# First products issued a slot early, piece sums on VectorE, interleaved weight conversion

## The chip, the core and the metric

The kernel runs on one core of a Trainium2 chip. The metric is device time in microseconds (us) of the whole kernel: 945.47 us, the median of three runs (941.27, 945.47, 945.98).

## What is computed

Three layers, one after the other, in float32 on the outside:

```python
attn_out = _attn_ref(q, k, v)                    # 4 x 8 heads, 576 x 64, masked softmax
x = attn_out.transpose(0, 2, 1, 3).reshape(2304, 512)
h = x @ w_in;  x = (h * cos(h)) @ w_out          # 512 -> 2048 -> 512
g = x @ w_gate                                   # 512 -> 1536
val = x @ w_val
out = (g / (1 + exp(-g)) * val) @ w_out2         # 1536 -> 512
```

## The kernel before

**Number format.** Each float32 matrix is scaled and split into two float16 parts, and a product takes three float16 matmuls in a row (`mm3`, lines 532 to 534, or line 680). "hi" is the rounded part, written by ScalarE (`hi_part` L245, `piece_hi` L654), "lo" is the rest, written by VectorE (`lo_part` L248, `piece_lo` L657).

**Stages.** The 2304 tokens are cut into five blocks, three of 512 and two of 384 columns (`BLOCKS`). After attention, the first dense layer runs as 5 x 16 steps: `up1` multiplies by a slice of `w_in`, ScalarE and VectorE form h cos(h) in four steps that alternate between them (L565 ScalarE, L568 VectorE, L572 ScalarE, L575 VectorE), L579 and L580 (POOL) split the result, and some steps later `down1` multiplies it by `w_out` into four accumulators `acc0` to `acc3`. A product of `up1` stays in a PSUM bank (the pool `bank` has four) until L575 of that step has read it.

**The second layer** uses a scheme with seven products in place of eight for 2 x 2 blocks, in both directions. It runs as 30 **slots** (5 blocks x 6). A slot makes seven products of four `mm3` each (`multiply(k, ...)`) with slice j of the gate and value weights, in the order 0, 1, 5, 4, 6, 2, 3. Some add to a bank that already holds an earlier product; before that, ScalarE copies the earlier state out (`snap`, L1170), and VectorE adds copies and banks up (`join`, L1174). `px`, `py` and `pz` are the three banks of a slot. From the joined gate and value halves come, for each of two row halves, a tanh (L643, ScalarE) and two VectorE steps (`silu`, L649 and L650). The first half is done inside its slot, the second half in the next slot. Then POOL forms four sums of quarters (`piece_sums`, L665), and hi and lo parts of the seven pieces are written (`first_set`: one piece; `second_set`: two; `third_set`: the four sums).

From slot 6 on, products of the block before with `w_out2` (`lower`, L680, seven a slot) fill TensorE between the products of a slot. They accumulate in `acc0` to `acc3` in turn (`k % KC`); `quarter_out` (L697, L703) empties them. In slots 0 to 5 there are none, except that slot 0 still has four `down1`. After slot 29 a **tail** of 42 `lower` for the last block remains.

**Work beside it.** Conversion of weights is kept in a list `fill`. Each item has a cost by hand, and `pump(share)` takes items until a budget is used up; in the first layer the budget is `SHARE` (0.95) of a step's slack in blocks 0 and 1 and `SHARE2` (0.77) from block `SB` = 2 on. The gate and value weights come first (POOL sums L902), then `w_out2`: twelve raw tiles of two 32-bit words a number, in six rounds j of two tiles. A round is `conv` (L224 ScalarE, L231 and L235 VectorE, for both tiles, then four sums on POOL, L323), `tops` (three hi parts in a row, ScalarE), `ends` (three lo parts, then `third`: a scaled copy of 1792 columns, L342, and the store to DRAM). All ScalarE items have cost 0, so that `pump` emits them in one go with the next item that has a cost.

A second list, `urgent`, holds for each block the scaling and splitting of the activations; `pump_urgent` takes one item. For the second layer these are eight **fold** items a block: items 0, 1, 5 and 6 contain a VectorE subtraction (L602), items 0 to 6 a hi part on ScalarE, items 1 to 7 a lo part on VectorE. The hi parts of items 5 and 6 read the difference of the same item. They are taken in slots 2 to 4 (three, three, two), and in the same place of the blocks that follow.

**What sets the order.** Every engine runs its own instructions in the order of emission; nothing is reordered by a scheduler. DMAs are issued on the SP queue in order of emission too. `load_w2` fetches slices of `w_out2` (576 KB) into the buffers in `w2_free`, `load_w7` a slot's gate and value weights (1792 KB) into one of three buffers.

## Time and profile before

| | |
|---|---|
| median of the three runs | 945.47 us |
| profiled execution, its own time | 940.64 us |
| span of its instructions | 938.9 us |
| TensorE busy | 870.9 us (93%) |
| VectorE busy | 669.8 us (71%) |
| ScalarE busy | 522.9 us (56%) |
| POOL busy | 301.3 us (32%) |

The span runs from the first to the last instruction of the profiled execution; its time is 1.7 us longer. Stretches below are given in us from the start of the span: the `w_out2` conversion lies in about 400 to 505, slots 0 to 5 in 518 to 603.7, slots 6 to 29 in 603.7 to 909, and the tail after that. A value in square brackets behind an instruction is the time for which its engine stood idle ahead of it and the instruction whose end released it.

### The profile page before, as it was taken

How to read it: one execution, taken by the hardware profiler on the slowest of the kernel's cores; microseconds unless marked ns; L12 is line 12 of the kernel's file. 1: busy time of each engine (PE TensorE's matmuls, PEld its weight loads, DVE VectorE, ACT ScalarE, POOL GpSimd, SP SyncE). 2: the span in 40 equal slices, each digit the busy share in tenths (PEclk: the TensorE clock that was granted, in tenths of full speed). 3: DMA queues.
4: the chain of work that ended last, by engine and by line, in shares of the span. 5: the costliest groups of instructions: out<-in, count | busy, mean ns of one | idle time of the engine just before them, and what ended most of it. 6: DMA issues, size and time to landing. Idle time of an engine off the chain costs nothing. (4 is left out here: it accounts for less than half of the span.)

```text
span 938.9 us, 18454 instructions
## 1 busy us (share of the span) xinstructions
PE 870.9 (93%) x7228; PEld 612.3 (65%) x7228; DVE 669.8 (71%) x1223; ACT 522.9 (56%) x1040; POOL 301.3 (32%) x367
## 2 busy tenths in 40 slices
PE   7999999989999799998789977899999999999997
PEld 4767644434444344554445666688888889999997
DVE  4898898976679979947686376657865775765662
ACT  4889888644365676546766455444434444444440
POOL 3344133112156656235452122212222122222220
PEclk7899999999999899999999997999999999999999
DMA  9998822475555746723545344457677768788866
GB/s 311 351 294 248 277 91 90 160 245 194 187 191 180 237 159 195 234 85 104 187 158 184 146 167 193 157 180 253 233 241 258 239 223 277 288 284 306 301 179 260
DMA packets 53511, 200.60 MB, mean 214 GB/s; under 512 B 5456, under 2 KB 16208, under 8 KB 49584
## 3 DMA queue, kind: packets, MB, share of 16 engines
q1 hardware_dynamic: 53424, 199.42, 62.3%
q8 instruction: 57, 0.93, 0.4%
q14 instruction: 30, 0.25, 0.1%
HBM read 175.41 MB, written 23.99 MB: 212 GB/s over the span
## 5 line engine op out<-in xcount | busy, mean ns | idle before, releaser
L532 PE MATMUL bank<-xs,wi 128*128 128x256 f16 (+3 forms) x860 | 258.3, 300 | 48.3 <-DVE tb L575 20.2
L533 PE MATMUL bank<-xs,wi 128*128 128x256 f16 (+3 forms) x860 | 258.0, 300 | 0.0
L534 PE MATMUL bank<-xs,wi 128*128 128x256 f16 (+3 forms) x860 | 257.8, 300 | 0.0
L580 POOL TENSOR_TENSOR arena<-tb,arena 128x512 f16<-128x512 f32 (+1 forms) x80 | 91.0, 1139 | 228.4 <-ACT arena L579 213.4
L533 PEld LDWEIGHTS <-wi 128*128 128x128 f16 x880 | 87.2, 99 | 91.1 <-issue 59.1
L665 POOL TENSOR_TENSOR wi<-tb 128x256 f32<-128x256 f32 (+1 forms) x60 | 40.6, 676 | 295.6 <-DVE tb L650 295.6
L533 PE MATMUL acc<-arena 128*128 128x512 f16 (+1 forms) x320 | 114.5, 358 | 0.4 <-POOL arena L580 0.4
L532 PE MATMUL acc<-arena 128*128 128x512 f16 (+1 forms) x320 | 114.5, 358 | 0.0
L534 PE MATMUL acc<-arena 128*128 128x512 f16 (+1 forms) x320 | 114.5, 358 | 0.0
L532 PEld LDWEIGHTS <-wi 128*128 128x128 f16 x880 | 87.3, 99 | 38.4 <-issue 3.8
L534 PEld LDWEIGHTS <-wi 128*128 128x128 f16 x880 | 87.4, 99 | 37.3 <-issue 3.0
L680 PEld LDWEIGHTS <-arena 128*128 128x128 f16 x1116 | 103.6, 98 | 8.6 <-DMA arena<-w 0.4
L1174 DVE TENSOR_TENSOR arena<-bank,cv 128x512 f32<-128x512 f32 (+1 forms) x90 | 57.0, 634 | 64.2 <-PE bank L534 56.7
L643 ACT ACTIVATE tb<-arena,c 128x512 f32<-128x512 f32 (+1 forms) x60 | 40.7, 679 | 95.8 <-DVE arena L1174 94.7
L565 ACT ACTIVATE tb<-bank,quarter,c 128x512 int32<-128x512 f32 (+1 forms) x75 | 54.4, 725 | 58.4 <-PE bank L534 42.3
L680 PE MATMUL acc<-arena 128*128 128x256 f16 (+1 forms) x750 | 86.3, 264 | 0.2 <-DMA arena<-w 0.2
L533 PEld LDWEIGHTS <-arena 128*128 128x128 f16 x600 | 59.0, 98 | 37.4 <-issue 4.5
L534 PEld LDWEIGHTS <-arena 128*128 128x128 f16 x600 | 59.0, 98 | 33.6 <-issue 0.6
L532 PEld LDWEIGHTS <-arena 128*128 128x128 f16 x600 | 59.0, 98 | 32.8
L532 PE MATMUL bank<-xs,arena 128*128 128x256 f16 (+1 forms) x280 | 74.1, 265 | 4.1 <-ACT cv L1170 4.1
L533 PE MATMUL bank<-xs,arena 128*128 128x256 f16 (+1 forms) x280 | 74.1, 265 | 0.0
L534 PE MATMUL bank<-xs,arena 128*128 128x256 f16 (+1 forms) x280 | 74.1, 265 | 0.0
(141 smaller groups left out, 1630.8 us busy)
## 6 DMA issues: line engine op xcount, KB each, us to landing
wi<-w SPq DMA_DIRECT2D x20, 1792.0 KB
arena<-w SPq DMA_DIRECT2D x62, 576.0 KB, 4.9
raw<-w_out SPq DMA_DIRECT2D x56, 512.0 KB, 4.3
arena<-w SPq DMA_DIRECT2D x10, 1792.0 KB
raw<-w_gate SPq DMA_DIRECT2D x24, 512.0 KB, 4.3
raw<-w_val SPq DMA_DIRECT2D x24, 512.0 KB, 5.0
w<-arena SPq DMA_DIRECT2D x42, 256.0 KB, 2.1
raw<-w_in SPq DMA_DIRECT2D x16, 512.0 KB
```

Source lines behind the costliest of these rows:

```text
L532: nc.tensor.matmul(out=o, lhsT=w[:, 0, c], rhs=x[0], start=first, stop=False, **kw)
L533: nc.tensor.matmul(out=o, lhsT=w[:, 0, c], rhs=x[1], start=False, stop=False, **kw)
L534: nc.tensor.matmul(out=o, lhsT=w[:, 1, c], rhs=x[0], start=False, stop=last, **kw)
L565: nc.scalar.activation(out=c["w"].bitcast(I32), in_=c["ph"], func=AF.Identity, scale=turn[c["blk"]], bias=quarter)
L580: nc.gpsimd.tensor_tensor(out=g[:, 1, 0:n], in0=w, in1=g[:, 0, 0:n], op=ALU.subtract)
L643: nc.scalar.activation(out=t, in_=c["C"][m][:, 0, 0:n], func=AF.Tanh, scale=half[c["blk"]])
L665: nc.gpsimd.tensor_tensor(out=to, in0=x, in1=y, op=ALU.subtract)
L680: nc.tensor.matmul(out=o[:, c], lhsT=w[:, 256 * i + 128 * c:256 * i + 128 * c + 128], rhs=unit(u)[:, x:x + h], start=j == c == i == 0, sto ...
L1174: nc.vector.tensor_tensor(out=c["C"][m][:, :, h * right:h * right + h], in0=p, in1=t, op=ALU.add)
```

## The change

Five edits.

1. **A slot's first product is issued a slot ahead.** `open_slot(s + 1)` takes a bank and issues product 0 of the next slot between products 6 and 3 of this one. The order inside a slot is now 1, 4, 5, 2, 6, (0 of the next slot), 3. `py` moves from the pool `bank` to `acc3`; `lower` therefore uses only `acc0` to `acc2` (`k % 3`), except for the first four products of the last block.
2. **Sums of pieces.** Three of the four sums of `piece_sums` move from POOL to VectorE. The first (`piece_first`) stays on POOL, a slot earlier, as soon as its inputs exist.
3. **The `w_out2` conversion** is cut into single steps and emitted with round j, j - 1 and j + 1 interleaved. Its four sums a round move from POOL to VectorE, with a cost of 0.45 each, and `third` is cut into 3 and 4 of 7 parts.
4. `SHARE2` rises from 0.77 to 0.85.
5. `load_w2` gets two freed weight buffers in slots 28 and 29 in place of after slot 29. The calls `pump(2.0)` and `pump(3.5)` in the slots are dropped; the list is empty there in both versions.

```diff
-SHARE, SHARE2, SB = 0.95, 0.77, 2
+SHARE, SHARE2, SB = 0.95, 0.85, 2
...
-                nc.gpsimd.tensor_tensor(out=sums[:, k], in0=x, in1=y, op=op)
+                nc.vector.tensor_tensor(out=sums[:, k], in0=x, in1=y, op=op)
...
+            def third(a, z):
+                nc.scalar.activation(out=stage[:, a:z, 512:768], in_=stage[:, a:z, 0:256], func=AF.Copy, scale=2.0 ** -11)
...
+                emit += now["fix"][0] + old["hi"][0:1] + now["fix"][1] + old["hi"][1:2] + now["sums"][0:2] + old["hi"][2:3]
+                emit += old["lo"][0:1] + now["sums"][2:4] + old["third"][0:1] + old["lo"][1:2] + new["conv"][0] + old["lo"][2:3]
+                emit += new["conv"][1] + old["third"][1:2] + old["store"]
...
-            for to, x, y in ((t1, b12, b11), (t3, b22, b12), (t2, b22, t1), (t4, b21, t2)):
-                nc.gpsimd.tensor_tensor(out=to, in0=x, in1=y, op=ALU.subtract)
+            for to, x, y in ((t2, b22, t1), (t3, b22, b12), (t4, b21, t2)):
+                nc.vector.tensor_tensor(out=to, in0=x, in1=y, op=ALU.subtract)
+
+        def piece_first(c):
+            h = c["n"] // 2
+            nc.gpsimd.tensor_tensor(out=t_sums[:, 0, 0:h], in0=c["t"][0][:, h:2 * h], in1=c["t"][0][:, 0:h], op=ALU.subtract)
...
-                acc_t[2, blk, k] = pacc.tile([128, 512], F32, name=f"acc{k % KC}")
+                acc_t[2, blk, k] = pacc.tile([128, 512], F32, name=f"acc{k if blk == NBLK - 1 and k < KC else k % 3}")
...
+        def open_slot(s):
+            blk, j = slots[s]
+            if j == 0:
+                need_urgent(("ys", blk))
+                up2_scales(blk)
+            h = BLOCKS[blk][1] // 2
+            p = halves(bank(), h)
+            multiply(0, w7_slots[s % W7S], ys[blk], p, h, True)
+            return p
...
+            if s + W7S > len(slots):
+                w2_free.extend(thirds((early_w[:, 0:14], early_w[:, 14:28], part(2 * HOMES, 14))[(s - 1) % W7S], 3))
+            if s == 4 or s + W7S > len(slots):
                 load_w2()
...
             a = snap(px)
+            while queue:
+                down_next()
+            py = halves(pacc.tile([128, 512], F32, name=f"acc{KC - 1}"), h)
             multiply(1, w, x, py, h, True)
             join(0, 0, py, a)
             if last:
+                piece_sums(last)
                 his, los = second_set(last)
                 run(his)
-            while queue:
-                down_next()
-            multiply(5, w, x, px, h, False)
-            a = snap(px)
+            pz = halves(bank(), h)
+            multiply(4, w, x, pz, h, True)
+            b = snap(pz)
             if last:
                 run(los)
             pump_urgent()
-            pz = halves(bank(), h)
-            multiply(4, w, x, pz, h, True)
-            b = snap(pz)
+            multiply(5, w, x, px, h, False)
+            a = snap(px)
...
-            multiply(6, w, x, px, h, False)
-            join(1, 1, px, b)
+            multiply(2, w, x, pz, h, False)
+            join(0, 1, pz, a)
             if last:
                 run(los)
             downs(2)
             pump_urgent()
-            pump(2.0)
-            multiply(2, w, x, pz, h, False)
-            join(0, 1, pz, a)
             t = gate_tanh(c, 0)
+            multiply(6, w, x, px, h, False)
+            join(1, 1, px, b)
             silu(c, 0, t)
             his, los = first_set(c)
             run(his)
+            piece_first(c)
             run(los)
+            old = px
+            if s + 1 < len(slots):
+                px = open_slot(s + 1)
             downs(3)
             pump_urgent()
-            pump(3.5)
-            multiply(3, w, x, px, h, False)
-            nc.scalar.activation(out=c["C"][1][:, :, 0:h], in_=px, func=AF.Copy)
+            multiply(3, w, x, old, h, False)
+            nc.scalar.activation(out=c["C"][1][:, :, 0:h], in_=old, func=AF.Copy)
```

**ScalarE in the conversion.** This is what stands between two steps of the first layer at a change of round before the change (L342 is `third`, L245 a hi part, L224 the first step of a tile, L565 the first step on a bank of `up1`):

```order
L342 ACTIVATE arena<-arena 128x7x256
L245 ACTIVATE arena<-raw,s_4741 128x256
L245 ACTIVATE arena<-raw,s_4741 128x2x256
L245 ACTIVATE arena<-arena,s_4741 128x4x256
L224 ACTIVATE raw<-raw 128x512
L565 ACTIVATE tb<-bank,quarter,c_4263 128x384
```

And this is what stands around one round's third and hi parts now (L336 is a part of `third`, L574, L588 and L581 are the steps that were L565, L579 and L572):

```order
L336 ACTIVATE arena<-arena 128x4x256
L245 ACTIVATE arena<-raw,s_4593 128x256
L574 ACTIVATE tb<-bank,quarter,c_4291 128x384
L588 ACTIVATE arena<-tb 128x384
L245 ACTIVATE xs<-xy_70,s_4719 128x384
L581 ACTIVATE tb<-tb,right 128x384
L245 ACTIVATE arena<-raw,s_4593 128x2x256
L574 ACTIVATE tb<-bank,quarter,c_4291 128x384
```

The block of `third`, three hi parts and the next tile's step, which stood ahead of L565 in a row, is spread over several steps of the first layer.

**TensorE between two slots.** The end of product 3 of slot 2 and the start of slot 3 before the change (weights from `arena` belong to slot 2, from `wi` to slot 3):

```order
L534 LDWEIGHTS arena_2101
L534 MATMUL bank_5931<-xs_5223,arena_2101 128x256
L532 LDWEIGHTS wi_71
L532 MATMUL bank_6055<-xs_5223,wi_71 128x256
L533 LDWEIGHTS wi_71
L533 MATMUL bank_6055<-xs_5223,wi_71 128x256
```

The same place now, one product earlier:

```order
L542 LDWEIGHTS wi_71
L542 MATMUL bank_6046<-xs_5235,wi_71 128x256
L543 LDWEIGHTS wi_71
L543 MATMUL bank_6046<-xs_5235,wi_71 128x256
L541 LDWEIGHTS arena_2101
L541 MATMUL bank_5924<-xs_5235,arena_2101 128x256
L542 LDWEIGHTS arena_2101
L542 MATMUL bank_5924<-xs_5235,arena_2101 128x256
```

Product 0 of slot 3 (bank_6046) is followed by product 3 of slot 2 (bank_5924), where it came after it.

**VectorE in a slot.** From the second half's silu to the last join of slot 1 before the change (L649 and L650 silu, L1174 join, L657 lo parts):

```order
L649 SCALAR_TENSOR_TENSOR tb<-tb,arena 128x512
L650 SCALAR_TENSOR_TENSOR tb<-tb,arena 128x512
L1174 TENSOR_TENSOR arena<-bank,cv 128x2x256
L657 SCALAR_TENSOR_TENSOR arena<-arena,tb 128x2x256
L1174 TENSOR_TENSOR arena<-bank,cv 128x2x256
L657 SCALAR_TENSOR_TENSOR arena<-arena,wi 128x4x256
L1174 TENSOR_TENSOR arena<-bank,cv 128x2x256
```

The same place now (L658 and L659 silu, L1190 join, L674 sums of pieces, L666 lo parts):

```order
L658 SCALAR_TENSOR_TENSOR tb<-tb,arena 128x512
L659 SCALAR_TENSOR_TENSOR tb<-tb,arena 128x512
L1190 TENSOR_TENSOR arena<-acc_5841,cv 128x2x256
L674 TENSOR_TENSOR wi<-tb,wi 128x256
L674 TENSOR_TENSOR wi<-tb 128x256
L674 TENSOR_TENSOR wi<-tb,wi 128x256
L666 SCALAR_TENSOR_TENSOR arena<-arena,tb 128x2x256
L1190 TENSOR_TENSOR arena<-bank,cv 128x2x256
```

Three sums stand between the first join and the lo parts, and the first join reads an accumulator in place of a bank.

**SP at the end.** Stores of the fourth block's output (L700) and loads of `w_out2` (L1102) around the last slots before the change:

```order
L700 DMA out<-xy_69 128x2x192
L1102 DMA arena<-w_0_2104 128x2304
L1102 DMA arena<-w_1_2105 128x2304
L700 DMA out<-xy_69 128x2x192
L1102 DMA arena<-w_0_2104 128x2304
L1102 DMA arena<-w_1_2105 128x2304
L700 DMA out<-xy_69 128x2x192
L1102 DMA wi<-w_0_2104 128x2304
```

And now (L713 and L1107):

```order
L1010 DMA arena<-w_5_2111 128x7168
L1107 DMA arena<-w_1_2105 128x2304
L1107 DMA arena<-w_0_2104 128x2304
L1107 DMA wi<-w_1_2105 128x2304
L1107 DMA wi<-w_0_2104 128x2304
L1107 DMA wi<-w_1_2105 128x2304
L1107 DMA arena<-w_0_2104 128x2304
L713 DMA out<-xy_69 128x2x192
```

The loads into `wi`, which came behind the last store of the fourth block, stand ahead of its second.

## Rows read from the trace of the kernel before

**Rows 1.** Windows: stretch, its us, busy us of PE, PEld, DVE, ACT, POOL; PEclk, DMA, GB/s
```profile
261.00:363.00 102.00, 95.48 (x433) 42.51 (x431) 89.72 (x139) 67.17 (x112) 59.46 (x58) 0.97 0.57 193
400.00:505.00 105.00, 88.67 (x510) 51.13 (x509) 70.19 (x125) 68.60 (x112) 47.30 (x46) 0.95 0.36 129
518.00:603.70 85.70, 70.77 (x568) 57.86 (x566) 51.38 (x80) 38.60 (x62) 20.16 (x24) 0.92 0.41 154
603.70:909.00 305.30, 296.43 (x3011) 275.05 (x3009) 202.19 (x334) 137.65 (x242) 75.41 (x96) 1.00 0.73 251
909.00:939.00 30.00, 23.26 (x258) 22.39 (x255) 8.74 (x15) 3.30 (x6) 2.52 (x4) 0.94 0.70 255
```

**Rows 2.** Waits of TensorE in 400 to 505: us in total, times, longest
```profile
PE bank L532 <- DVE tb L575: 14.2, 8, 3.8
```

**Rows 3.** Timeline: POOL's first of four sums, then ScalarE, TensorE
```profile
419.31 0.85 POOL L323 TENSOR_TENSOR arena<-raw 128x256 f32<-128x256 f32 x1 [1.78 <-DVE raw L235]
...
422.50 1.15 ACT L245 ACTIVATE arena<-arena,s 128x1024 f16<-128x1024 f32 x1 [2.48 <-POOL arena L323]
...
427.54 0.48 PE L532 MATMUL bank<-xs,wi 128*128 128x384 f16 x1 [3.83 <-DVE tb L575]
```

**Rows 4.** Timeline of ScalarE and VectorE at another change of round
```profile
449.37 1.69 ACT L342 ACTIVATE arena<-arena 128x1792 f16<-128x1792 f16 x1
...
453.74 0.43 DVE L231 TENSOR_SCALAR raw<-raw 128x512 int32<-128x512 int32 x1 [5.14 <-ACT raw L224]
```

**Rows 5.** Windows, of line 323 (POOL's sums) alone
```profile
400.00:505.00 105.00, 25.84 (x24) 0.95 0.36 129
```

**Rows 6.** Waits of TensorE in 518 to 604, then in 604 to 909
```profile
PE bank L532 <- ACT cv L1170: 14.8, 5, 4.4
...
PE bank L532 <- ACT cv L1170: 8.9, 8, 1.8
```

**Rows 7.** Timeline from slot 4 to slot 5, VectorE, ScalarE and TensorE
```profile
587.20 1.22 DVE L657 SCALAR_TENSOR_TENSOR arena<-arena,wi 128x1024 f16<-128x1024 f16 x1
...
588.99 0.68 DVE L1174 TENSOR_TENSOR arena<-bank,cv 128x512 f32<-128x512 f32 x1
589.71 0.72 ACT L643 ACTIVATE tb<-arena,c 128x512 f32<-128x512 f32 x1 [2.96 <-DVE arena L1174]
590.46 0.69 DVE L649 SCALAR_TENSOR_TENSOR tb<-tb,arena 128x512 f32<-128x512 f32 x1 [0.79 <-ACT tb L643]
...
591.91 0.42 ACT L654 ACTIVATE arena<-tb 128x256 f16<-128x256 f32 x1 [1.48 <-DVE tb L650]
...
593.48 0.58 ACT L1170 ACTIVATE cv<-bank 128x512 f32<-128x512 f32 x1
594.10 0.37 PE L532 MATMUL bank<-xs,arena 128*128 128x256 f16 x1 [2.38 <-ACT cv L1170]
```

**Rows 8.** Timeline of slot 4's folds: VectorE alone, then beside POOL
```profile
577.87 0.68 DVE L602 TENSOR_TENSOR wi<-xy 128x512 f32<-128x512 f32 x1
...
582.76 2.34 POOL L665 TENSOR_TENSOR wi<-tb,wi 128x256 f32<-128x256 f32 x2
583.30 1.22 DVE L602 TENSOR_TENSOR wi<-xy,wi 128x512 f32<-128x512 f32 x1
```

**Rows 9.** Windows of slots 1 to 5, of slot 2, of slot 3
```profile
535.30:602.40 67.10, 52.26 (x423) 43.71 (x421) 45.41 (x65) 33.03 (x54) 17.74 (x20) 0.90 0.46 173
546.90:558.00 11.10, 9.35 (x86) 8.22 (x85) 8.09 (x12) 6.86 (x11) 3.68 (x4) 1.00 0.48 167
558.00:574.00 16.00, 12.05 (x87) 9.50 (x85) 10.61 (x16) 7.43 (x12) 3.68 (x4) 0.79 0.31 116
```

**Rows 10.** Timeline: VectorE empties an accumulator of the first layer, slot 0
```profile
528.51 0.62 DVE L546 TENSOR_SCALAR xy<-acc,c 128x384 f32<-128x384 f32 x1 [0.36 <-PE acc L534]
```

**Rows 11.** Timeline of the tail: SP issues loads, TensorE waits
```profile
911.37 4.29 SPq L1102 DMA_DIRECT2D wi<-w  x6
...
917.44 0.67 PE L680 MATMUL acc<-arena,wi 128*128 128x192 f16 x6 [2.62 <-DMA wi<-w]
```

More of the change, by code (lines that the diff above doesn't have):

```diff
@@ L303, in direct_later, with seven_steps @@
             rests.append((0.7, lambda: lo_part(tiles[j][:, 1], box["c"], scale_w[mat][0], tiles[j][:, 0]), (mat, j)))
[L305 to L323 removed]
+        def seven_steps(j, stage, sums):
+            boxes, conv = [], []
+            for q in range(2):
+                box, steps = conv_steps("out2", 2 * j + q, None, False, lambda: None)
+                boxes.append(box)
+                conv.append(steps)
             def sources():
@@ L343, in third, with store @@
+            def store():
                 nc.sync.dma_start(out=w2_d[j // 3][:, :, j % 3].rearrange("q p n -> p q n"), in_=stage)
-            def tops():
-                for k in range(3):
-                    later(0, lambda k=k: hi(k))
-            def ends():
-                for k, cost in ((2, 1.25), (1, 0.7), (0, 0.45)):
-                    later(cost, lambda k=k: lo(k))
-                later(0, third, ("out2", j))
-            return conv, tops, ends
+            return dict(conv=[c[0:1] for c in conv], fix=[c[1:] for c in conv],
+                        sums=[(0.45, lambda k=k: combine(k)) for k in range(4)],
+                        hi=[(0, lambda k=k: hi(k)) for k in range(3)],
+                        lo=[(cost, lambda k=k: lo(k)) for k, cost in enumerate((0.45, 0.7, 1.25))],
+                        third=[(0, lambda: third(0, 3)), (0, lambda: third(3, 7))], store=[(0, store, ("out2", j))])
@@ new lines, in seven_later @@
+        def seven_later():
+            all_steps = [seven_steps(j, *stages[j % 2]) for j in range(NPR)]
+            none = dict(conv=[[], []], fix=[[], []], sums=[()] * 4, hi=[()] * 3, lo=[()] * 3, third=[()] * 2, store=[()])
+            emit = []
+            for a in all_steps[0]["conv"]:
+                emit += a
+            for j in range(NPR + 1):
+                now = all_steps[j] if j < NPR else none
+                old = all_steps[j - 1] if j else none
+                new = all_steps[j + 1] if j + 1 < NPR else none
+                emit += now["fix"][0] + old["hi"][0:1] + now["fix"][1] + old["hi"][1:2] + now["sums"][0:2] + old["hi"][2:3]
+                emit += old["lo"][0:1] + now["sums"][2:4] + old["third"][0:1] + old["lo"][1:2] + new["conv"][0] + old["lo"][2:3]
+                emit += new["conv"][1] + old["third"][1:2] + old["store"]
+            for step in emit:
+                if step:
+                    later(*step)
@@ L944, in open_weights @@
                 scale_later("out2", TW_LAST)
-                ends = None
-                for j in range(NPR):
-                    conv, tops_, next_ends = seven_later(j, *stages[j % 2])
-                    conv()
-                    if ends:
-                        ends()
-                    tops_()
-                    ends = next_ends
-                ends()
+                seven_later()
         opened, most = [], [HOMES]
@@ L1147, in build @@
             h = n // 2
-            if j == 0:
-                need_urgent(("ys", blk))
-                up2_scales(blk)
             if s == 1:
@@ L1228, in build @@
         blk = NBLK - 1
-        for i in range(len(slots) - W7S, len(slots) - 1):
-            w2_free.extend(thirds((early_w[:, 0:14], early_w[:, 14:28], part(2 * HOMES, 14))[i % W7S], 3))
         c_last[blk] = prod(c_o[blk], scale_w["out2"][1])
```

32 lines of the change are left out of this document (8 added, 24 removed).

## The prediction

> **What bounds the kernel now.** I read the busy time by stretch first, then who TensorE waited for in each, then the timeline in front of the longest waits. TensorE is the bound: it is busy 93% of the span, and from 604 to 909 it works 296.4 of 305.3 us [rows 1]. So the change can only win TensorE's idle time and what the low clock level costs. That sits in four places, all read from [rows 1, 2, 6, 11]. In the conversion (400 to 505) TensorE idles 105 - 88.7 = 16.3 us, 14.2 of them for VectorE's L575, which frees the bank, and a mean granted clock of 0.95 costs about 0.05 x 105 = 5.2 us more. In slots 0 to 5 it waits 14.8 us for ScalarE's copy L1170, and 0.08 x 85.7 = 6.9 us go to the clock. In slots 6 to 29 it waits 8.9 us for the same copy. In the tail it waits 2.6 us for a load, and 0.06 x 30 = 1.8 us go to the clock. Together 55 us; the question is how much of each place comes back.
>
> **The conversion (edits 2 and 3).** Two things hold up the bank. Four sums run on POOL one after the other, from 419.31 on; the hi part of the sums waits for them 2.48 us on ScalarE, and the four-step chain on the banks is queued behind it, so TensorE starts 3.83 us late [rows 3]. At another round ScalarE does `third` (1.69), three hi parts and the next tile's step in a row, and VectorE sits idle for 5.14 us [rows 4]. Both go: the order shows the ScalarE burst spread over several steps, and the sums come a round ahead of their use. What is new: 24 sums on VectorE. No row has one of 256 columns there; the nearest has 512 columns and takes 0.68 us [rows 8], so each costs between 0 and 0.68, and I take 0.40, near half: 24 x 0.40 = 9.6 us. VectorE is busy 70.2 us in a stretch that would shrink to some 91 us: (70.2 + 9.6) / 91 = 88%; ScalarE 68.6 / 91 = 75%. Neither is the bound by itself, but both are full enough for some waits to stay. The common scales and the two-chain cross waits stay as well. I keep 4 of the 14.2 us and a quarter of the clock's 5.2: **gain 10.2 + 3.9 = 14 us**, bounds 4 (VectorE full) and 18 (all but the scales).
>
> **SHARE2 (edit 4)** moves work, it adds none. In block 2 VectorE is already busy 89.7 of 102 us and TensorE loses 6.5 [rows 1]. About a tenth more conversion a step fills VectorE further there and empties block 3. I take **0**, bounds -5 (about the loss that is there doubled) and +4.
>
> **Slots 0 to 5 (edits 1 and 2).** The wait is a chain, readable from slot 4 to slot 5 [rows 7]: after product 2, join (588.99, 0.68), tanh (0.72), silu (twice 0.69), hi part (0.42), copy of product 3, tanh of the second half (0.72 again), copy of `px` (593.48, 0.58), and only then product 5. From 588.99 to 594.06 that is 5.1 us. Beside it TensorE has products 3, 0 and 1, and a product takes 9.35 / 7 = 1.3 us [rows 9], so 3.9 us: TensorE waits. After the change five products stand between 2 and the next 5 (6, 0 of the next slot, 3, 1, 4), 6.6 us. The chain gets longer too, because the lo part of the third set (1.22 for 1024 columns) and the join after product 6 (0.68) stand ahead of silu on VectorE: I work it out to some 6.1 us after product 2. It fits, barely. One new wait appears: the copy of `pz` is queued on ScalarE behind the second set's hi parts, which wait for silu, so product 2 starts about 0.4 us late. A slot without folds thus takes 7 x 1.31 + 0.4 = 9.6 us.
>
> Slots with folds are worse. VectorE has to do the three sums (1.2 us) and, in slots 2 to 4, up to three fold items of 0.7 to 1.4 us, and the join that product 3 waits for is queued behind one of them: about 1.4 us of wait in slot 2, 0.9 in slot 3. In slot 4 the hi part of fold item 6 needs its own VectorE subtraction and stands on ScalarE ahead of the copy that frees `px` for product 6. There I count four waits, of 1.7, 0.8, 1.7 and 0.8 us. That makes slots of 11.0, 11.2 and 14.1 us, and 9.6 and 10.1 us for slots 1 and 5: 56 us against 67.1 now [rows 9], a gain of 11. Slot 0 gives 0.6 back: product 1 goes to `acc3` and must wait until VectorE has emptied it (0.62 us after the last `down1`) [rows 10]. I leave 1.5 us for one stretch of the low clock. **Gain 9 us**, bounds 2 and 15. The sums cost VectorE 1.2 us a slot, but POOL's sums stretch its work now: L602 takes 0.68 us alone and 1.22 beside L665 [rows 8], so most of that comes back in slots with folds.
>
> **Slots 6 to 29.** Seven `lower` a slot, 0.67 us each by the tail's row [rows 11], add 4.7 us of cover; about five of them lie over the chain, so it has 6.6 + 3.3 = 9.9 us of TensorE work beside it, and the fold slots still fit. Of 8.9 us I keep 3.9: **gain 5**, bounds 1 and 7. Three accumulators in place of four cost nothing within a block, since two whole products lie between two uses of one.
>
> **The tail (edit 5).** Six loads are issued at 911.37, and TensorE waits for one until 917.44 [rows 11]. SP's order has them two slots earlier, over 10 us. The wait of 2.6 us and most of the low clock after it go. Against that, `acc0` now holds both the fourth block's last product and the first one of the tail, and the `quarter_out` between them comes behind silu: about 0.7 us. **Gain 3.5**, bounds 2 and 4.5. Piece loads of SP queued behind these early ones have a slot's time of slack.
>
> **The sum:** 14 + 0 + 9 + 5 + 3.5 = 31.5 us off the profiled execution's 940.6 gives 909. The three runs' median is 4.8 us above that execution; I set the forecast at 911, between 909 and 945.5 - 31.5 = 914.
>
> **Rivals.**
> *Everything fits (12%).* All bounds at the good end: 18 + 4 + 15 + 7 + 4.5 = 48 us, about 894. For it: the waits have few causes. Against it: the four waits counted in slot 4 are in the order.
> *The conversion gains next to nothing (17%).* VectorE becomes the bound there. The sums read two operands from SBUF, and POOL's L580 remains beside them; if each of some 20 steps stretches VectorE by as much as L602 was stretched (0.54), then (70.2 + 9.6 + 11) / 91 is 100%. Gain 3 in place of 14: 922. Against it: 26 us of POOL work with the same effect leave [rows 5]. The Trainium skill, "SBUF — State Buffer", Who interferes with whom, says that a VectorE instruction with two SBUF inputs and a GpSimd instruction that reads SBUF lock each other out; the trace agrees with 1.22 against 0.68 us [rows 8], and by that rule the moved sums are exposed to it too.
> *The slots gain nothing (10%).* The ScalarE queue in fold slots (hi part ahead of the copy) holds product 6 longer than I count, and a low clock stretch stays: gain 0 and 2 in place of 9 and 5: 923.
> *Nearly all of it at once (4%).* Conversion 3, block 2 -5, slots 0 and 2, tail 3.5: 939, no change.
> *Slower than before (5%).* Many short waits keep TensorE at its low level. Slot 3 had a mean clock of 0.79 and took 16.0 us, slot 2 with 1.00 took 11.1 [rows 9]. A slot at the low level costs another 9.35 us, and about 2 us of waits vanish under it, so five slots of it cost 5 x (9.35 - 2) = 37 us, which is the point where it decides; through slot 6 (9.35 + 4.7 = 14 us more) the time is 911 + 37 + 14 = 962. Against it: slot 2 waits 11.1 - 9.35 = 1.8 us and stays at 1.00. The Trainium skill, "TensorE: Matmul & The Clock Gate", A second HAM failure mode: psum-queue depth-cycling, describes just such short pauses between groups with the clock going back and forth; here slot 2 at 1.00 speaks against it, slot 3 for it, and by the rule fold slots would stay low.
>
> **How the numbers follow.** The forecast has 52%. A measurement here tells about 0.5% (4.7 us) from no change. Faster by more is the forecast, the first three rivals: 91%. Same 4%, slower 5%. The range reaches from near the good end, 896, to past the two rivals at 922 and 923, to 930: outside remain the last two rivals and slivers at both ends.
>
> **What would show it.** Right: between 400 and 500 TensorE's wait for L575 drops to about 4 us with VectorE near 88% busy and POOL under 25%; slots without folds take 9.6 us and slot 4 still about 14, with waits ahead of products 6 and 3 in place of 5; no wait for `wi` in the tail. Wrong: VectorE over 95% in the conversion with the waits for L575 still there, a mean clock under 0.9 in slots 1 to 5, or a wait of the tail that only moves to another load.

## The result and the profile after

The changed kernel takes 900.62 us (median of four runs, 900.30 to 904.13) against 945.73 us for the kernel before beside it; the ratio is 0.9536, with a 95% interval from 0.9494 to 0.9579. The forecast was 911 in a range of 896 to 930: the sign and the range hold, and the gain is larger than forecast: 45.1 us between the medians, and 41 us by stretches (below) where the working had 31.5.

The profiled execution of the changed kernel is the slowest of its four runs (904.13 us, span 902.2), that of before was at the fast end of its own (940.64). So I compare stretch by stretch. The table cuts the span of each profiled kernel where TensorE has issued the same number of matmuls; "conversion" runs from the ninth step of block 3 to the last `down1` but four, "slots 0 to 5" on to product 1 of slot 6, and the tail begins with the end of slot 29's products. The columns add up to the span; all times are us, worked out from the traces. The other kernels are those of the experiments below.

| kernel | ahead of block 2 | block 2 | block 3 to step 8 | conversion | slots 0 to 5 | slots 6 to 29 | tail | span |
|---|---|---|---|---|---|---|---|---|
| before | 261.1 | 102.2 | 37.0 | 116.0 | 87.4 | 305.5 | 29.6 | 938.9 |
| **after** | 265.6 | 104.4 | 38.4 | 96.4 | 76.8 | 295.1 | 25.7 | 902.2 |
| after_again | 271.4 | 104.1 | 38.4 | 96.4 | 76.8 | 295.1 | 25.7 | 907.8 |
| c_sums_pool | 260.6 | 106.1 | 37.1 | 101.7 | 76.8 | 295.1 | 25.7 | 902.9 |
| c_burst | 273.1 | 105.7 | 38.0 | 114.1 | 76.8 | 295.1 | 25.7 | 928.4 |
| c_sums_twice | 261.4 | 105.4 | 39.6 | 101.5 | 76.8 | 295.1 | 25.7 | 905.5 |
| a_share79 | 261.4 | 102.8 | 37.4 | 96.2 | 85.5 | 295.1 | 25.7 | 904.1 |
| late_open | 260.9 | 105.1 | 38.0 | 96.4 | 80.3 | 295.2 | 25.7 | 901.6 |
| pieces_pool | 260.4 | 105.3 | 40.0 | 96.4 | 79.2 | 295.1 | 25.7 | 901.9 |
| old_order | 261.7 | 105.5 | 39.7 | 96.4 | 88.1 | 318.1 | 26.4 | 935.8 |
| fold_pool | 266.9 | 105.4 | 37.1 | 96.3 | 77.5 | 295.5 | 25.7 | 904.3 |
| late_w2 | 260.5 | 104.2 | 38.4 | 96.4 | 76.8 | 295.1 | 26.9 | 898.3 |
| fold0 | 264.1 | 104.8 | 37.1 | 96.4 | 71.2 | 295.1 | 25.7 | 894.3 |
| fold0_share83 | 266.4 | 104.4 | 36.5 | 95.5 | 71.2 | 295.1 | 25.7 | 894.7 |

Two things are to be seen. From the conversion on, a stretch that an edit leaves alone repeats to 0.1 us or so from kernel to kernel, so one profile tells a microsecond there. And the work ahead of block 2, which no edit touches, varies by 13 us. The two traces of the changed kernel (after and after_again) differ by 5.6 us in all and by 5.8 there; that the medians scatter for the same reason is likely, but only traces show it. Blocks 2 and 3 scatter as well, by less: in the eleven traces with the share of 0.85 the two together take 141.9 to 145.3 us. Leaving the work ahead of block 2 aside, the change gave, in the order of the columns: -2.2 - 1.4 + 19.6 + 10.6 + 10.4 + 4.0 = 41.0 us, and 940.6 - 41.0 = 899.6 agrees with the median of 900.6.

The windows of the changed kernel for block 2, conversion, slots 0 to 5, slots 6 to 29 and tail (columns as in [rows 1]; the last cut lies 0.3 us later than in the table):

```profile
265.56:369.93 104.37, 95.39 (x434) 42.63 (x433) 96.86 (x147) 69.91 (x117) 64.21 (x64) 0.97 0.63 211
408.33:504.70 96.37, 93.86 (x578) 56.34 (x576) 82.52 (x153) 74.14 (x126) 24.64 (x25) 1.00 0.49 175
504.70:581.51 76.81, 68.25 (x578) 56.24 (x576) 54.75 (x97) 39.21 (x66) 7.27 (x10) 1.00 0.42 153
581.51:876.83 295.32, 295.32 (x3014) 275.34 (x3012) 213.67 (x405) 136.63 (x243) 16.59 (x25) 1.00 0.78 272
876.83:902.20 25.37, 20.95 (x253) 20.72 (x251) 8.45 (x17) 3.05 (x5) 0.00 (x0) 0.98 0.53 168
```

And who TensorE waited for (us in total, times, longest), in the conversion, in slots 0 to 5 and in the tail; in slots 6 to 29 the view has no row at all:

```profile
PE bank L541 <- DVE q L137: 1.8, 2, 1.4
PE bank L541 <- DVE tb L584: 0.7, 1, 0.7
...
PE bank L541 <- ACT cv L1186: 5.3, 7, 1.5
PE bank L541 <- DVE arena L1190: 2.5, 3, 1.2
PE acc L541 <- DVE xy L555: 0.7, 1, 0.7
...
PE acc L693 <- DVE xy L710: 0.7, 1, 0.7
```

Against [rows 2] the wait for the step that frees the bank (L584, L575 before) fell from 14.2 to 0.7 us, with VectorE at 82.5 / 96.4 = 86%. Against [rows 6] the wait for the copy L1186 (L1170 before) fell from 14.8 to 5.3 us in slots 0 to 5 and from 8.9 to none in slots 6 to 29, where TensorE is busy for the whole stretch. The clock is 1.00 in the conversion (0.95 before) and in slots 0 to 5 (0.92 before).

### The profile page after: what moved, and what is told of

Its sections match the earlier page's. It is cut to its first block, busy times and chain, and to the rows that moved or that the text cites. A ratio compares the mean times of both kernels' runs of the same rounds, so it can differ in the third digit from the quotient of the medians.

```text
span 902.2 us, 18542 instructions
## 1 busy us (share of the span) xinstructions
PE 862.4 (96%) x7228; PEld 609.8 (68%) x7228; DVE 691.8 (77%) x1337; ACT 521.2 (58%) x1046; POOL 199.3 (22%) x253
## 4 chain that ended last, share of the span: by engine, by line
PE 66%; DVE 10%; ACT 7%; DMA 6%; issue 6%; POOL 4%; SPq 0%; POOLq 0%; ACTq 0%; DVEq 0%
PE acc L693 14%; PE bank L541 10%; PE bank L543 10%; PE bank L542 10%; PE acc L541 5%; PE acc L543 5%; PE acc L542 5%; DMA vl<-v_l 3%; PE bank L435 2%; DVE arena L248 2%; POOL arena L915 2%; POOL arena L589 2%; PE po L488 2%; ACT arena L245 2%; DMA v_pair<-v_s 1%
## 5 line engine op out<-in xcount | busy, mean ns | idle before, releaser
L541 PE MATMUL bank<-xs,wi 128*128 128x256 f16 (+3 forms) x780 | 233.8, 300 | 22.1 <-DVE tb L584 9.1
L543 PE MATMUL bank<-xs,wi 128*128 128x256 f16 (+3 forms) x780 | 234.1, 300 | 0.0
L542 PE MATMUL bank<-xs,wi 128*128 128x256 f16 (+3 forms) x780 | 233.9, 300 | 0.0
L542 PEld LDWEIGHTS <-wi 128*128 128x128 f16 x880 | 86.2, 98 | 62.5 <-issue 30.2
L541 PEld LDWEIGHTS <-wi 128*128 128x128 f16 x880 | 86.3, 98 | 38.4 <-issue 4.1
L543 PEld LDWEIGHTS <-wi 128*128 128x128 f16 x880 | 86.3, 98 | 35.6 <-issue 1.4
L693 PEld LDWEIGHTS <-arena 128*128 128x128 f16 x1080 | 100.7, 98 | 8.2
L678 POOL TENSOR_TENSOR wi<-tb 128x256 f32<-128x256 f32 (+1 forms) x30 | 20.2, 675 | 347.5 <-DVE tb L659 347.5
L663 ACT ACTIVATE arena<-tb 128x256 f16<-128x256 f32 (+3 forms) x59 | 28.9, 489 | 115.3 <-DVE tb L659 111.6
L574 ACT ACTIVATE tb<-bank,quarter,c 128x512 int32<-128x512 f32 (+1 forms) x75 | 54.4, 725 | 49.5 <-PE bank L543 36.9
L542 PEld LDWEIGHTS <-arena 128*128 128x128 f16 x600 | 58.8, 98 | 35.0 <-issue 2.5
L693 PE MATMUL acc<-arena 128*128 128x256 f16 (+1 forms) x702 | 82.0, 265 | 0.0
L543 PEld LDWEIGHTS <-arena 128*128 128x128 f16 x600 | 58.7, 98 | 33.0 <-issue 0.2
L541 PEld LDWEIGHTS <-arena 128*128 128x128 f16 x600 | 58.8, 98 | 32.8 <-ACT arena L588 0.3
L658 DVE SCALAR_TENSOR_TENSOR tb<-tb,arena 128x512 f32<-128x512 f32 (+1 forms) x60 | 38.0, 634 | 44.9 <-ACT tb L652 44.8
L588 ACT ACTIVATE arena<-tb 128x512 f16<-128x512 f32 (+1 forms) x80 | 46.5, 581 | 35.4 <-PE acc L543 32.4
L541 PE MATMUL bank<-xs,arena 128*128 128x256 f16 (+1 forms) x240 | 62.9, 262 | 1.7 <-DVE arena L1190 1.2
L543 PE MATMUL bank<-xs,arena 128*128 128x256 f16 (+1 forms) x240 | 62.9, 262 | 0.0
```

The source lines that it names most:

```text
L541: nc.tensor.matmul(out=o, lhsT=w[:, 0, c], rhs=x[0], start=first, stop=False, **kw)
L542: nc.tensor.matmul(out=o, lhsT=w[:, 0, c], rhs=x[1], start=False, stop=False, **kw)
L543: nc.tensor.matmul(out=o, lhsT=w[:, 1, c], rhs=x[0], start=False, stop=last, **kw)
L574: nc.scalar.activation(out=c["w"].bitcast(I32), in_=c["ph"], func=AF.Identity, scale=turn[c["blk"]], bias=quarter)
L588: nc.scalar.activation(out=g[:, 0, 0:n], in_=w, func=AF.Copy)
L658: nc.vector.scalar_tensor_tensor(out=t, in0=t, scalar=1.0, in1=gate, op0=ALU.add, op1=ALU.mult)
```

## Experiments on the conversion

Theory: the order of the steps makes the gain. Rival: the engine that does the sums makes it. Each of the first two kernels undoes one half in the changed kernel.

**c_sums_pool**: the four sums on POOL again, in the new order.

```diff
-                nc.vector.tensor_tensor(out=sums[:, k], in0=x, in1=y, op=op)
+                nc.gpsimd.tensor_tensor(out=sums[:, k], in0=x, in1=y, op=op)
...
-                        sums=[(0.45, lambda k=k: combine(k)) for k in range(4)],
+                        sums=[(0, lambda k=k: combine(k)) for k in range(4)],
```

> The changed kernel with one thing undone: the four sums of a conversion round are back on POOL, at cost 0; the interleaved order stays. Stretch looked at: from the ninth step of block 3 to the last down1 that is not a slot's, 96.4 us in the changed kernel and 116.0 before. Theory (the order of the steps makes the gain, because no engine meets a burst of another one): the stretch stays within 3 us of 96.4, since the sums are a round ahead of their use, and VectorE falls from 86% to about 72% busy. Rival (taking the sums off POOL makes the gain): the stretch goes back to 104 us or more, with waits of ScalarE's hi part for POOL of 2 us as before.

Measured: 101.7 us, between theory and rival; 905.89 us median, ratio 0.9601 (0.9538 to 0.9664). TensorE's waits in the stretch:

```profile
PE bank L541 <- DVE q L137: 4.6, 2, 2.4
PE bank L541 <- DVE tb L584: 1.5, 2, 1.1
```

Of the 5.3 us that this costs, 0.8 are more waiting for the bank, 2.8 are the two common scales (a reduction on VectorE, L137), which both kernels have but which meet other work here (at cost 0 the budget also takes the conversion faster), and the rest goes with the clock at 0.98. The old wait for POOL's sums doesn't come back. So the engine is worth about 5 us in the new order, and hardly any of that through the wait that I read in [rows 3].

**c_burst**: the old order again, with the sums on VectorE.

```diff
-                emit += now["fix"][0] + old["hi"][0:1] + now["fix"][1] + old["hi"][1:2] + now["sums"][0:2] + old["hi"][2:3]
-                emit += old["lo"][0:1] + now["sums"][2:4] + old["third"][0:1] + old["lo"][1:2] + new["conv"][0] + old["lo"][2:3]
-                emit += new["conv"][1] + old["third"][1:2] + old["store"]
+                for c, f in zip(now["conv"], now["fix"]):
+                    emit += c + f
+                emit += now["sums"] + old["lo"][::-1] + old["third"] + old["store"] + now["hi"]
```

> The changed kernel with the other half undone: the sums stay on VectorE (0.45 each), but the steps of a round stand again in the old order, both tiles' conversion, the sums, the lo parts and the whole of third for the round before, then three hi parts. Same stretch, 96.4 us changed and 116.0 before. Theory (order): bursts come back, the stretch takes 106 to 114 us, with waits of TensorE for the step that frees the bank of 8 us or more. Rival (engine): the stretch stays under 100 us.

Measured: 114.1 us; 925.79 us median, ratio 0.9791 (0.9723 to 0.9858). The theory stands: with the old order and the sums on VectorE, 17.7 of the 19.6 us are lost again, and what the engine gives in the old order is 1.9 us (116.0 before, with the smaller share, against 114.1). TensorE's wait, and the burst on ScalarE in its timeline (start, us; L336 is `third`, L245 a hi part, L224 the next tiles' first step; the steps on the bank stand three lines higher than in the changed kernel, so L581 is what was L584):

```profile
PE bank L538 <- DVE tb L581: 10.3, 5, 2.9
```

```profile
435.68 1.77 ACT L336 ACTIVATE arena<-arena 128x768 f16<-128x768 f16 x2
437.36 1.15 ACT L245 ACTIVATE arena<-raw,s 128x256 f16<-128x256 f32 x2
438.41 1.13 ACT L245 ACTIVATE arena<-arena,s 128x1024 f16<-128x1024 f32 x1
439.45 1.24 ACT L224 ACTIVATE raw<-raw 128x512 f32<-128x512 f32 x2
```

This is [rows 4] once more: some 5 us of ScalarE in a row, behind which the steps on the bank stand. The work is the same in both kernels, and in the changed one it costs nothing, because it lies a piece at a time between those steps.

**c_sums_twice** computes each sum a second time, to see how much room VectorE has left:

```diff
                 nc.vector.tensor_tensor(out=sums[:, k], in0=x, in1=y, op=op)
+                nc.vector.tensor_tensor(out=sums[:, k], in0=x, in1=y, op=op)
```

> The changed kernel with each of the 24 sums of the conversion computed twice on VectorE (the second time with the same result), at the same budget. That adds 24 x 0.53 = 12.8 us to the 82.5 us that VectorE is busy in the stretch of 96.4 us, 95.3 in all. Theory (in the interleaved order the bank's wait comes from bursts, and VectorE has room up to nearly its full time): the stretch grows by 3 us or less. Rival (at 86% VectorE is already close to its bound, so what is added shows in the time): it grows by 8 to 13 us.

Measured in a single run: 101.5 us, 5.1 more, between theory and rival.

```profile
406.50:508.00 101.50, 95.65 (x577) 56.73 (x576) 91.77 (x177) 74.30 (x126) 23.79 (x25) 0.98 0.45 166
```

```profile
PE bank L542 <- DVE q L137: 3.9, 2, 2.9
PE bank L542 <- DVE tb L585: 1.9, 3, 0.9
```

VectorE is busy 9.3 us more (91.8 of 101.5, 90%), and 3.3 us of new waits and a clock of 0.98 follow. So at 86% there was some room, but not 10 us of it: about half of what was added shows.

**a_share79**: SHARE2 at 0.79.

```diff
-SHARE, SHARE2, SB = 0.95, 0.85, 2
+SHARE, SHARE2, SB = 0.95, 0.79, 2
```

> The changed kernel with SHARE2 at 0.79 in place of 0.85. Block 2 took 102.2 us before (0.77) and 104.4 to 106.1 in the kernels with 0.85. Theory (the larger share fills VectorE, 93% busy there, and costs time): block 2 takes 101 to 103.5 us, and the stretch of the conversion stays within 1.5 us of 96.4, since conversion ended some 15 us ahead of the slots. Rival (the difference in block 2 is where the common scales fall, not the share): block 2 stays at 104 us or more, or what it gains is lost in block 3 or in the conversion.

Measured: block 2 102.8, conversion 96.2, but slots 0 to 5 85.5 us; 907.42 us median, ratio 0.963 (0.9572 to 0.9688). The last steps of the conversion now come behind slot 0, too late, and the kernel no longer computes what the others do; its times are read all the same. The last store of converted weights is issued by SP at 523.19, in slot 1. ScalarE's hi part of that slot (L663) waits 5.9 us for this store to be done, the copy of `pz` is queued behind the hi part, and TensorE waits once for 5.5 us:

```profile
523.19 0.36 SPq L339 DMA_DIRECT2D w<-arena  x1
```

```profile
ACT arena L663 <- DMA w<-arena: 5.9, 1, 5.9
```

```profile
PE bank L541 <- ACT cv L1186: 10.8, 7, 5.5
```

Block 2 is the fastest of all kernels with the edit, as the theory had it, but the larger share is what pays for the sums: without it slots 0 to 5 lose 8.7 us, three times the 2.8 that blocks 2 and 3 and the conversion give back.

## Experiments on the slots and the tail

**old_order** puts products 5 and 4, and 6 and 2, back into the old order.

```diff
-            pz = halves(bank(), h)
-            multiply(4, w, x, pz, h, True)
-            b = snap(pz)
...
             multiply(5, w, x, px, h, False)
             a = snap(px)
...
+            pz = halves(bank(), h)
+            multiply(4, w, x, pz, h, True)
+            b = snap(pz)
...
-            multiply(2, w, x, pz, h, False)
-            join(0, 1, pz, a)
...
             multiply(6, w, x, px, h, False)
             join(1, 1, px, b)
...
+            multiply(2, w, x, pz, h, False)
+            join(0, 1, pz, a)
```

> The changed kernel with the order inside a slot put back: 1, 5, 4, 6, 2, (0 of the next slot), 3 in place of 1, 4, 5, 2, 6, (0), 3. The early first product, acc3 and the sums on VectorE stay. Theory (the order of the products is the cover that made the gain of the slots): slots 0 to 5 take 82 us or more in place of 76.8, and slots 6 to 29 lose 5 us or more against 295.1, with waits of TensorE for the copy of px ahead of product 5. Rival (the early product and the sums made it): both within 2 us of the changed kernel.

Measured: 88.1 and 318.1 us, no faster than before in slots 0 to 5 and 12.5 us slower in slots 6 to 29; 937.22 us median, ratio 0.9934 (0.9899 to 0.9969). Waits in slots 0 to 5, then in 6 to 29:

```profile
PE bank L541 <- ACT cv L1186: 14.7, 5, 4.4
...
PE bank L541 <- ACT cv L1186: 19.1, 24, 1.8
```

None of the slots' gain is left without the order, and with the old order the other edits even cost 12.5 us in slots 6 to 29; which of them does was not tried. With product 2 near the end of the slot only 0, 3 and 1 lie between it and the next 5, and the chain behind it doesn't fit, in slots 6 to 29 not even once (24 waits in 24 slots).

**late_open** keeps the new order and issues product 0 in its own slot again.

```diff
             old = px
-            if s + 1 < len(slots):
-                px = open_slot(s + 1)
...
+            if s:
+                px = open_slot(s)
             if last:
                 t = gate_tanh(last, 1)
```

> The changed kernel, but each slot's first product is issued at the start of its own slot again, behind product 3 of the slot before; the new order of the others (1, 4, 5, 2, 6, 3), the bank in acc3 and the sums on VectorE stay. Between product 2 and the next slot's product 5 stand five products either way. Theory (the order of the other products made the gain of the slots, the early first product adds nothing): slots 0 to 5 and slots 6 to 29 both stay within 2 us of the changed kernel's 76.8 and 295.3 us. Rival (the early product is the cover): 5 us or more are lost in slots 0 to 5, and waits of TensorE for the copy of px come back in slots 6 to 29.

Measured: 80.3 us (+3.5) and 295.2 us (no change); 906.47 us median, ratio 0.9597 (0.9547 to 0.9647). Neither side has it whole. Its waits in slots 0 to 5:

```profile
PE bank L541 <- DVE arena L1190: 9.5, 6, 2.5
PE bank L541 <- ACT cv L1186: 2.2, 3, 1.4
```

What the early product covers is another wait than the one I had it for: product 3 adds to the bank that the join behind product 6 must have read, and product 0 of the next slot between the two hides 7 us of that (9.5 against 2.5), while the wait for the copy is 3.1 us shorter in late_open (2.2 against 5.3). In slots 6 to 29 three `lower` stand there anyway, and the early product is worth nothing.

**pieces_pool**: the three sums of pieces on POOL again.

```diff
-                nc.vector.tensor_tensor(out=to, in0=x, in1=y, op=ALU.subtract)
+                nc.gpsimd.tensor_tensor(out=to, in0=x, in1=y, op=ALU.subtract)
```

> The changed kernel with the three sums of pieces back on POOL, where the first sum stays early. Theory (the sums' engine matters little where the product order gives cover): slots 6 to 29 stay at 295 to 297 us, and slots 0 to 5 stay within 3 us of 76.8, since what POOL takes longer than VectorE, VectorE gets back at 1.2 us a slot. Rival (the sums on POOL hold up the third set's hi part on ScalarE and stretch VectorE's steps beside them): slots 0 to 5 take 82 us or more and waits show in slots 6 to 29, 4 us or more.

Measured: 79.2 us (+2.4) and 295.1 us; 902.91 us median, ratio 0.9552 (0.9501 to 0.9603), as the theory had it.

**late_w2** loads the last weights after slot 29 again.

```diff
-            if s + W7S > len(slots):
-                w2_free.extend(thirds((early_w[:, 0:14], early_w[:, 14:28], part(2 * HOMES, 14))[(s - 1) % W7S], 3))
-            if s == 4 or s + W7S > len(slots):
+            if s == 4:
                 load_w2()
...
         blk = NBLK - 1
+        for i in range(len(slots) - W7S, len(slots) - 1):
+            w2_free.extend(thirds((early_w[:, 0:14], early_w[:, 14:28], part(2 * HOMES, 14))[i % W7S], 3))
```

> The changed kernel without the early release of two weight buffers in slots 28 and 29: their loads come after slot 29 again. Only the tail is looked at, from the end of slot 29, 25.7 us in the changed kernel and 29.6 before. Theory (the loads' place is the whole gain of the tail): the wait for wi of 2.6 us and a stretch of the low clock come back, and the tail takes 28.5 to 29.7 us. Rival (the tail gained from the accumulators or from what VectorE has left to do at its start): it stays under 27 us.

Measured: 26.9 us, 1.2 more than with the edit and 2.7 less than before; 900.55 us median, ratio 0.955 (0.9486 to 0.9614). Its waits in the tail:

```profile
PE acc L693 <- DMA wi<-w: 0.8, 2, 0.6
PE acc L693 <- DVE xy L710: 0.7, 1, 0.7
```

The wait for `wi` was 2.6 us in one piece before [rows 11]. Here it is 0.8 in two, and the clock in this tail is 1.00 (0.94 before [rows 1]). So the rival stands, by 0.1 us: edit 5 is worth 1.2 us, and 2.7 came with other edits. The loads here are issued at 872.74, 1.4 us after the tail's start against 2.1 before, and TensorE starts on the first of them 5.3 us later against 6.1; what made them quicker wasn't tried apart.

**fold_pool** moves the folds' subtractions (L611) to POOL, since the waits that are left sit in slots 2 to 4. TensorE's waits of slot 4 in the changed kernel, and ScalarE and VectorE ahead of the first of them:

```profile
561.94 0.27 PE L541 MATMUL bank<-xs,wi 128*128 128x256 f16 x1 [1.47 <-ACT cv L1186]
...
564.06 0.27 PE L541 MATMUL bank<-xs,wi 128*128 128x256 f16 x1 [0.65 <-ACT cv L1186]
...
566.96 0.27 PE L541 MATMUL bank<-xs,wi 128*128 128x256 f16 x1 [1.43 <-ACT cv L1186]
...
570.43 0.27 PE L541 MATMUL bank<-xs,wi 128*128 128x256 f16 x1 [0.69 <-DVE arena L1190]
```

```profile
558.73 0.68 DVE L611 TENSOR_TENSOR wi<-xy 128x512 f32<-128x512 f32 x1
...
559.45 0.72 ACT L245 ACTIVATE xs<-wi,s 128x512 f16<-128x512 f32 x1 [1.34 <-DVE wi L611]
560.08 0.58 ACT L1239 ACTIVATE arena<-bank 128x512 f32<-128x512 f32 x1
560.69 0.72 ACT L652 ACTIVATE tb<-arena,c 128x512 f32<-128x512 f32 x1
561.32 0.58 ACT L1186 ACTIVATE cv<-bank 128x512 f32<-128x512 f32 x1
```

The hi part waits for its subtraction, and the copy of product 3, the tanh and the copy of `px` are queued behind it.

```diff
             def sub(out, a, b):
-                nc.vector.tensor_tensor(out=out, in0=a, in1=b, op=ALU.subtract)
+                nc.gpsimd.tensor_tensor(out=out, in0=a, in1=b, op=ALU.subtract)
```

> The changed kernel with the subtractions of the fold items (L611) on POOL, which is 7% busy in slots 1 to 5, in place of VectorE. Theory (the waits that are left in slots 2 to 4, about 6 us, come from the fold's hi part, which stands on ScalarE ahead of the copy of px or of product 3 and waits for its own subtraction, queued on VectorE): slots 0 to 5 take 70 to 74.5 us in place of 76.8. Rival (POOL is so much slower, or stretches VectorE's steps so much, that the hi parts come no earlier): 76 us or more.

Measured: 77.5 us, 0.7 more; 901.63 us median, ratio 0.9571 (0.9512 to 0.9629). The rival stands. POOL takes twice as long, and the two steps of silu beside it are stretched:

```profile
537.56 1.46 POOL L611 TENSOR_TENSOR wi<-xy 128x512 f32<-128x512 f32 x1
...
538.46 1.11 DVE L658 SCALAR_TENSOR_TENSOR tb<-tb,arena 128x512 f32<-128x512 f32 x1 [0.57 <-ACT tb L652]
539.10 1.60 POOL L611 TENSOR_TENSOR wi<-xy,wi 128x512 f32<-128x512 f32 x1
539.60 1.64 DVE L659 SCALAR_TENSOR_TENSOR tb<-tb,arena 128x512 f32<-128x512 f32 x1
```

Alone these two take 0.69 us each [rows 7].

**fold0 and fold0_share83**: what can't move to another engine can move in time. VectorE is busy 48 us in slots 1 to 5 of the changed kernel (9.0, 9.8, 9.9, 11.2, 8.0), where TensorE's products need 46.8 (five slots at the 9.35 us of [rows 9]); in slot 0, beside the last `down1`, it is busy 5.0 of 17.7. So the folds of block 1 go there:

```diff
+            if s == 0:
+                urge(fold_pieces(1, sy, ys, spans), ("ys", 1))
             while queue:
                 down_next()
+                pump_urgent()
+                pump_urgent()
...
-            if j == 1 and blk + 1 < NBLK:
+            if j == 1 and 0 < blk < NBLK - 1:
                 urge(fold_pieces(blk + 1, sy, ys, spans), ("ys", blk + 1))
```

> The changed kernel with the fold items of block 1 taken in slot 0 (two behind each of its four down1, the rest at its three places) in place of slots 2 to 4. In slots 1 to 5 VectorE is busy 48 us and TensorE's products need 46.8, so VectorE has no room there; in slot 0 it is busy 5.0 of 17.7 us. Theory (what is left in slots 1 to 5 is VectorE's and ScalarE's work for the folds): slots 2 to 4 take some 9.7 to 10.3 us each as slots 1 and 5 do, slots 0 to 5 come to 70 to 72 us in place of 76.8, and the kernel is 4 to 7 us faster than the changed one. Rival (the folds only move the wait: the first layer's accumulators are emptied later in slot 0, and the chain from product 2 to product 5 is late without folds too): slots 0 to 5 stay over 75 us.

The second has SHARE2 at 0.83 as well; and the changed kernel ran once more beside both.

> As fold0, and SHARE2 at 0.83 in place of 0.85. Theory (share): block 2 falls to 103 to 104.5 us, the conversion still ends ahead of the slots, and 1 to 2 us more are gained. Rival (block 2 depends on where the common scales fall, not on the share): block 2 stays at 104 us or more and nothing is gained.

> The changed kernel itself once more, beside the next two on the same chip. Slots 0 to 5 should take 76.8 us and the conversion 96.4 us again, since these stretches differed by less than 0.1 us between kernels that leave them alone; what varies lies ahead of block 2.

Measured on one chip: 905.94 us for the changed kernel (ratio to before 0.9559, 0.9502 to 0.9617), 896.57 for fold0 (0.9495, 0.944 to 0.9551) and 892.34 for fold0_share83 (0.9445, 0.9399 to 0.9492). So fold0_share83 beats the changed kernel, with intervals that don't touch; those of fold0 and the changed kernel overlap a little. Slots 0 to 5 take 71.2 us in both. The windows of slots 0 and 1 of the changed kernel, then of slots 0, 1 and 2 of fold0:

```profile
507.70:525.35 17.65, 16.94 (x133) 12.76 (x132) 5.04 (x11) 4.96 (x7) 1.32 (x3) 1.00 0.00 1
525.35:535.65 10.30, 9.63 (x87) 8.23 (x85) 9.03 (x18) 5.49 (x9) 0.73 (x1) 1.00 0.50 178
```

```profile
505.30:523.30 18.00, 17.20 (x134) 12.83 (x133) 11.47 (x24) 9.10 (x14) 1.30 (x3) 1.00 0.00 1
523.30:534.70 11.40, 9.64 (x87) 8.23 (x85) 9.95 (x16) 5.73 (x10) 0.73 (x1) 1.00 0.44 161
534.70:544.40 9.70, 9.49 (x86) 8.22 (x85) 7.98 (x14) 5.50 (x9) 0.73 (x1) 1.00 0.53 191
```

VectorE takes 6.4 us more in slot 0, and the slot grows by only 0.3 us. Slot 1 grows by 1.1, to 11.4: the last lo part of the folds falls into it, and TensorE waits 1.8 us for ScalarE's copies there (0.6 in the changed kernel). Slots 2 to 5 take 9.7 us each, and 5.6 of the 76.8 us are gone, as the theory had it. That is the part of fold0's gain that the traces show for sure; its median is 9.4 us below that of the changed kernel.

The share of 0.83 gives 0.4 in block 2, 0.6 in block 3 and 0.9 in the conversion, 1.9 in all. Only the last is clear of the scatter of its stretch; blocks 2 and 3 together take 140.9 us, 1.0 below the lowest trace with 0.85. Block 2 at 104.4 lies in the theory's range and in the rival's, so this trace doesn't decide between them, and the medians of fold0 and fold0_share83 have overlapping intervals. Of the 13.6 us between the medians of the changed kernel and fold0_share83, the stretches of the two traces account for 8.1 (5.6 in slots 0 to 5, 0.9 in the conversion, 1.9 in block 3, -0.3 in block 2), the 1.9 within the scatter of block 3; the two traces differ by another 5.0 ahead of block 2.

## Why the prediction came out as it did

**The mechanisms held, their sizes were too small.** Each place named as the source of the gain gave one. By stretches the sum fell short by 9.5 us: 5.6 in the conversion, 5.4 in slots 6 to 29, 1.6 in slots 0 to 5 and 0.5 in the tail, less the 3.6 that blocks 2 and 3 lost.

**The conversion: 14 forecast, 19.6 measured, bounds 4 to 18.** The step that failed is the sum's last: "I keep 4 of the 14.2 and a quarter of the clock's 5.2". What stayed is 0.7, and the clock stayed at 1.00, with no wait for the bank over 0.7 us. The load was forecast well (88% of VectorE; 86% came out, POOL at 26%), but two errors cancel in it. A sum took 0.53 us on average where I took 0.40. And VectorE's other work got shorter, which stood among the rivals but not in the sum: with the sums on POOL and VectorE's other instructions the same (c_sums_pool) it is busy 79.8 us there, so that the 12.5 us of sums add only 2.7 to it. What I had wrong is what that load means: 82.5 us of work in 96.4 doesn't make waits by itself once nothing stands in bursts. The rival by which VectorE would be the bound is not far off, though: c_sums_twice loses 5.1 us at 90%. And the two causes that I named weigh very differently: the bursts are 17.7 us by c_burst, POOL's sums at most 5.3.

**SHARE2: 0 forecast, -2.2 in block 2 and -1.4 in block 3 measured.** This is inside the bounds, on the side of the loss; by the scatter of the eleven traces with 0.85 (141.9 to 145.3 against 139.2 before) the two blocks lost between 2.7 and 6.1. a_share79 shows the edit's other side: at the smaller share the conversion reaches into the slots.

**Slots 0 to 5: 9 forecast, 10.6 measured.** The working by slots holds: 9.6, 11.0, 11.2, 14.1 and 10.1 us were forecast for slots 1 to 5, and 10.3, 10.9, 11.0, 14.0 and 9.7 were measured, 55.9 for 56.0 in all. That the sums agree to 0.1 is luck: slot 1 was 0.7 too short and slot 5 0.4 too long, and the 11.2 of slot 3 doesn't follow from its terms (9.6 and a wait of 0.9 make 10.5). The four waits of slot 4 were counted at 1.7, 0.8, 1.7 and 0.8 and measured at 1.47, 0.65, 1.43 and 0.69. One place is wrong: I had product 5 free of waits, and the first of the four is still ahead of it. Slot 0's wait for `acc3` is 0.71 (0.6 forecast). The 1.5 us kept for a low clock weren't needed: that is nearly the whole difference. And the cover was put down to two edits where one makes it: the order of the products (old_order), while the early product is worth 3.5 us by another wait (late_open) and the sums 2.4.

**Slots 6 to 29: 5 forecast, 10.4 measured, bounds 1 to 7.** "Of 8.9 us I keep 3.9" had no row behind it. The step that failed is that one: the chain of 6.1 us and the 9.9 us of cover stood beside it, and taken at their word they leave no wait; none is left. The other 1.5 us are TensorE's own busy time, 295.3 for 296.9.

**The tail: 3.5 forecast, 4.0 measured, for a reason that is only in part mine.** The new wait behind `quarter_out` is there, 0.71 us as forecast. But edit 5 is worth 1.2, not the whole of it, so that the size came out near is luck; what made the other 2.7 stays open.

**The rival of the low clock.** Slots 2 to 4 have waits of 0.6 to 1.5 us in every slot and stay at 1.00; in old_order, with waits of up to 4.4 us, slots 0 to 5 have a mean clock of 0.92. The Trainium skill, "TensorE: Matmul & The Clock Gate", A second HAM failure mode: psum-queue depth-cycling, would have had the slots with short pauses going back and forth; here it doesn't show at pauses of this size. The forecast's "would stay low" went further than that section.

## What to carry to other kernels

Where one engine feeds a bound one through a chain, count the work of the bound engine that lies between the chain's two ends in the order of issue, and reorder before moving anything to another engine: here the order of seven products and of conversion steps made most of the gain, and the change of engine 2 to 5 us. If cover and chain are both read from rows and the cover is half as long again, forecast the wait as gone. What can't change its engine may change its time: here an engine's spare time in the stage before was cheaper than another engine's (5.6 us gained in fold0, 0.7 lost in fold_pool).
